# Score products on 64 contraction rows, with q and k turned over unsplit, in an attention and FFN kernel

## The chip, the cores and the metric

One core of a Trainium2 chip runs the whole program. The metric is device time in microseconds of one execution, the median of several runs. TensorE (PE) multiplies and transposes, VectorE (DVE), ScalarE (ACT) and GpSimd (POOL) do the element-wise work, SyncE (SP) issues the DMAs.

## The reference, cut to what matters

Inputs are q, k, v of 2 batches, 8 heads, 768 positions and 64 features, all float32, a projection of 64 x 6, and the weights of two FFNs.

```python
q_bits = (einsum('bhsd,dk->bhsk', q, proj) > 0); k_bits likewise
q_bucket = sum(q_bits * 2**arange(6)); k_bucket likewise
mask = q_bucket[:, :, :, None] == k_bucket[:, :, None, :]
scores = where(mask, q @ k.T / sqrt(64), -1e9)
attn = softmax(scores) @ v                       # per head, 768 x 64
x = attn of all heads side by side               # 1536 x 512
x = leaky_relu(x @ w_in, 0.01) @ w_out           # 512 -> 2048 -> 512
x = (max(h, 0) + alpha * min(h, 0)) @ w_out2     # h = x @ w_in2
```

The result has to be near float32. The kernel gets this from narrower products: a number is held as a rounded high part and the low part that is left, and a product is the sum of high x high, high x low and low x high.

## The kernel before, in words

**Tiles and loops.** The attention goes over 8 pairs of heads (`pairs`, i = 0 to 7). A pair has 12 score tiles, one for each head j of two and each block of 128 query rows (two halves f of three blocks t); a tile is 128 x 768. `TILES` (line 30) is the order of the six (t, j) of a half. The FFNs follow (`ffn`, line 1396); the conversion of their float64 weights (`convert`) runs partly beside the attention.

**The order of the work.** Every step is handed to a planner with a claim (its place in a nominal order), a duration for the planner, what it reads and what it writes (`plan.add`). `Plan.order` lists the steps of each engine by these and improves the order by passes over the whole program; `emit` writes it out. Each engine then runs its own list in order and waits on semaphores. A `ring` is a set of slots that successive buffers take in turn; a buffer waits until the slot's last one has been read.

**A pair's q and k.** `load` (482) brings the two heads of k, q and v, 128 positions on the partitions, 768 numbers each. `split_qk` (542) makes high and low parts ("nat"), by GpSimd for all pairs but the first (lines 470, 473). `turn` (584) transposes them on TensorE (line 597): 128 columns of a head, 64 high and 64 low, become 128 contraction rows, 24 transposes of 128 x 128 for a pair. ScalarE evicts them from PSUM (line 612) into "qa" and "ka", in which the parts lie in opposite order, so that one product over 128 rows gives high x low plus low x high. "qb" and "kb" hold the high parts alone on 64 rows, a copy made by DMA (line 622), and 12 more rows with sign bits.

**The sign bits.** `bits` (631) multiplies the projection (`lhs`, each number and its negative) with the split tiles on 128 rows (line 640): four products side by side on quarters of the columns, for two halves. VectorE compares (line 649), and DMAs lay the bits behind "qb" and "kb" (line 659). For the first pair, copies by the engines stand in for the DMAs (lines 612, 616, 671 and 672). Bits that differ add large terms to the score (`BIG`), which is how the mask enters.

**Scores.** `score` (752) has for each tile two products of 128 rows and two of 76 rows, 384 columns each (line 768), into one of two PSUM slots (`s_ps`). VectorE takes the row minimum and moves the tile to SBUF (line 775), ScalarE takes the exponential (778). Then the tile is turned over: "T" tiles by TensorE (794) and ScalarE (799), the others as high and low halves (812, 818, 470, 473) by a DMA transpose (824). `HI_ON`, `LO_ON` and their `_END` forms say which way each of the 12 tiles takes and which engine does it. `pv` (829) multiplies with v (864, 873) and scales the output (885).

**Buffers.** PSUM has two slots for transposes, bits and others (`t_ps`), one for outputs, one for tiles turned over and two (of two banks each) for scores. The slots of q and k serve the FFN's x later (`op_at`, 952).

Of the kernel before, what the change touches and what calls it, by code (L numbers as in the profile page):

```python
# [18 lines left out]
BIG = 2.0**33  # L19
# [10 lines left out]
TILES = ((0, 0), (2, 0), (0, 1), (1, 0), (2, 1), (1, 1))  # L30
HI_ON = "ATATTTATPATP"
LO_ON = "P-D---P-DP-D"
HI_END, LO_END = "ATATTTATATTT", "P-D---P-D---"
# [17 lines left out]
START, XAT = 10.0, (1, 9)  # L51

# [303 lines left out]
def lsh_attention_ffn_kernel(  # L356
# [66 lines left out]
    op_r = dict(zip(("qa", "qb", "ka", "kb"), ring("op", 4, ("qa", "qb", "ka", "kb"))))  # L423
# [17 lines left out]
    lhs = fixed([128, 32], F32, "lhs")  # L441
    least = fixed([128, 1], F32, "least")
    weight = fixed([128, 1], F32, "weight")
    pj = fixed([128, NB], F32, "pj")
    x_t = {}
# [33 lines left out]
    st_raw, st_nat, st_op, st_bt, st_v = {}, {}, {}, {}, {}  # L479
    sums, pts, st_v32 = {}, {}, {}  # L480

    def load(i, nm, claim, parts=1):
        b, hp = pairs[i]
        src = {"q": q, "k": k, "v": v}[nm][b, 2 * hp:2 * hp + 2]
        t = (rv_r if nm == "v" else raw_r[nm]).new([128, 2, T, D], F32, nm)
        st_raw[nm, i] = t
        for n in range(parts):
            js = slice(2 * n // parts, 2 * (n + 1) // parts)
            plan.add(
                claim,  # L490
                dma(2.4 / parts, lambda js=js: t.t[:, js],
                    lambda js=js: src[js].rearrange("j (p t) d -> p j t d", t=T)),
                writes=[(t, (js.start, js.stop))],
            )

    def setup():
# [8 lines left out]
        def masks():  # L505
            nc.gpsimd.memset(lhs.t, 0.0)
            nc.gpsimd.memset(least.t, 0.0)
            for g in range(4):
                rows = slice(32 * g, 32 * g + 32)
                nc.gpsimd.memset(weight.t[rows], BIG if g % 2 else 1.0)  # L510
                nc.gpsimd.affine_select(
                    out=least.t[rows],
                    in_=least.t[rows],
                    compare_op=ALU.is_ge,
                    fill=-TINY,
                    base=-NB if g % 2 else NB - 1,
                    pattern=[[0, 1]],
                    channel_multiplier=1 if g % 2 else -1,
                )

        plan.add(-98, gps(3.0, masks), writes=[lhs, least, weight])

        def projections():
            for c in range(2):
                gmul(lhs.t[:, NB * c:NB * c + NB], pj.t, -1.0 if c else 1.0)
# [16 lines left out]
    def split_qk(i, parts):  # L542
        for nm, hi, at in (("k", 1, -15), ("q", 0, -13)):
            raw = st_raw.pop((nm, i))
            nat = nat_r[nm].new([128, 2, T, 2, D], F32R, nm + "n")
            st_nat[nm, i] = nat
            for part in range(parts):
                js = slice(2 * part // parts, 2 * (part + 1) // parts)
                u = 1 / parts

                def views(js=js, raw=raw, nat=nat, hi=hi):
                    r = raw.t[:, js].rearrange("p j t d -> p (j t) d")
                    n = nat.t[:, js].rearrange("p j t a d -> p (j t) a d")
                    return n[:, :, hi], n[:, :, 1 - hi], r

                def d_hi(v=views):
                    h, _, r = v()
                    nc.vector.tensor_copy(h, r)

                def a_hi(v=views):  # L560
                    h, _, r = v()
                    nc.scalar.copy(out=h, in_=r)

                def p_hi(v=views):
                    h, _, r = v()
                    gmul(h, r, 1.0)

                def d_lo(v=views):
                    h, lo, r = v()
                    vsub(lo, r, h.bitcast(F32))  # L570

                def p_lo(v=views):
                    h, lo, r = v()
                    gsub(lo, r, h.bitcast(F32))

                span = (js.start, js.stop)
                hi_ways = [vec(0.62 * u + 0.05, d_hi, True), act(0.65 * u + 0.18, a_hi), gps(0.8 * u + 0.05, p_hi)]
                plan.add(12 * i + at, hi_ways if parts > 1 else hi_ways[2], [(raw, span)], [(nat, span)])
                lo_ways = [vec(0.9 * u + 0.05, d_lo, True), gps(1.787 * u + 0.05, p_lo)]
                plan.add(  # L580
                    12 * i + at + 1, lo_ways if parts > 1 else lo_ways[1], [(raw, span)], [(nat, span)]
                )

    def turn(i):
        ops = [{nm: op_r[nm].new([128, S], F32R, nm) for nm in op_r} for j in range(2)]
        st_op[i] = ops
        at = 12 * i - 12
        for nm, hi, sc in (("k", 64, -scale), ("q", 0, 1.0)):
            n = st_nat.pop((nm, i))
            for j in range(2):  # L590
                a, bb = ops[j][nm + "a"], ops[j][nm + "b"]
# [909 lines left out]
```

## Time and profile before

| | |
|---|---|
| Median of 3 runs | 729.72 us (728.97 to 730.33) |
| The profiled execution | 728.91 us, span of its instructions 727.1 us |
| TensorE busy | 708.4 us (97%) |
| VectorE busy | 603.2 us (83%) |
| ScalarE busy | 473.9 us (65%) |
| GpSimd busy | 311.7 us (43%) |
| TensorE's granted clock | full throughout |

Busy times of TensorE count overlapping matmuls once, but each matmul's record is longer than the time after which the next can follow; how far two starts lie apart tells more than the length of one. The chain that ended last follows the work back from the last instruction, at each step to what released it; its shares say which engine the end hangs on. A group of instructions has its busy time, the mean of one, and the idle time of its engine just before it, with what ended that.

### The profile page before, as it was taken

What the parts mean: (1) busy time and instruction counts of PE and PEld (TensorE: products, weight loads), DVE (VectorE), ACT (ScalarE), POOL (GpSimd) and SP (SyncE); (2) the same over time, 40 slices, a digit from 0 to 9 for tenths busy, and PEclk for the clock granted to TensorE, in tenths of its full rate; (3) what the DMA queues carried; (4) which work ended last, traced back from release to release, by engine and by line L of the source; (5) the groups of instructions that cost most, each with busy time, mean ns of one, the idle gap of its engine ahead of it and who ended that gap; (6) DMA issues with size and microseconds to landing.
All of it is one profiled execution on the core that took longest, in us unless ns stands there. A gap on an engine that the chain in (4) does not pass through costs nothing.

```text
span 727.1 us, 13418 instructions
## 1 busy us (share of the span) xinstructions
PE 708.4 (97%) x5113; PEld 461.6 (63%) x5113; DVE 603.2 (83%) x1094; ACT 473.9 (65%) x896; POOL 311.7 (43%) x325
## 2 busy tenths in 40 slices
PE   7999999999998999999999999999999999999997
PEld 5788898888887666666666666555555555555553
DVE  5888887887799989869989878999989999987442
ACT  4888897887897776756656555564776655636340
POOL 1866776868562165132533422424043335323220
PEclk9999999999999999999999999999999999999999
DMA  7457889777565230331322314021132203100012
GB/s 218 109 140 183 166 160 179 173 145 172 118 131 160 87 116 13 106 116 58 103 72 88 95 52 117 6 71 41 59 101 73 88 30 117 58 1 1 24 50 102
DMA packets 103281, 70.86 MB, mean 97 GB/s; under 512 B 72928, under 2 KB 95456, under 8 KB 103216
## 3 DMA queue, kind: packets, MB, share of 16 engines
q1 hardware_dynamic: 103216, 70.00, 36.6%
q8 instruction: 40, 0.66, 0.4%
q14 instruction: 25, 0.20, 0.1%
HBM read 43.00 MB, written 3.15 MB: 63 GB/s over the span
## 4 chain that ended last, share of the span: by engine, by line
PE 72%; DVE 20%; ACT 3%; issue 3%; POOL 1%; DMA 1%; SPq 0%; POOLq 0%; DVEq 0%; ACTq 0%
PE y L1233 10%; PE y L1235 10%; PE y L1234 10%; PE sc L768 7%; PE h L1233 7%; PE h L1234 7%; PE h L1235 7%; PE pp L794 5%; PE o L873 4%; DVE ff L1157 3%; PE o L864 3%; PE tp L597 2%; DVE s L775 2%; DVE ff L1070 2%; DVE x L1367 2%
## 5 line engine op out<-in xcount | busy, mean ns | idle before, releaser
L473 POOL TENSOR_TENSOR ff<-ff 128x384 f16<-128x384 f32 x128 | 137.0, 1084 | 196.8 <-ACT ff L1267 161.1
L1233 PE MATMUL y<-ff 128*128 128x384 f16 (+1 forms) x496 | 172.0, 347 | 0.0
L1235 PE MATMUL y<-ff 128*128 128x384 f16 (+1 forms) x496 | 171.9, 347 | 0.0
L1234 PE MATMUL y<-ff 128*128 128x384 f16 (+1 forms) x496 | 171.9, 347 | 0.0
L1233 PE MATMUL h<-ff 128*128 128x384 f16 x416 | 135.7, 326 | 1.1 <-DVE ff L1278 1.0
L1235 PE MATMUL h<-ff 128*128 128x384 f16 x416 | 135.6, 326 | 0.3 <-DVE ff L1157 0.3
L1234 PE MATMUL h<-ff 128*128 128x384 f16 x416 | 135.6, 326 | 0.0
L1234 PEld LDWEIGHTS <-ff 128*128 128x128 f16 x912 | 89.3, 98 | 69.8 <-issue 2.6
L1235 PEld LDWEIGHTS <-ff 128*128 128x128 f16 x912 | 89.2, 98 | 69.8 <-DVE ff L1157 0.6
L1233 PEld LDWEIGHTS <-ff 128*128 128x128 f16 x912 | 89.2, 98 | 68.3
L775 DVE TENSOR_SCALAR_CACHE_REDUCE s<-sc 128x768 f32<-128x768 f32 x96 | 90.9, 954 | 13.5 <-PE sc L768 10.3
L778 ACT ACTIVATE s<-s,mn 128x768 f32<-128x768 f32 x96 | 90.0, 940 | 8.7 <-DVE s L775 7.6
L1267 ACT CAST ff<-ff 128x384 f16<-128x384 f32 x128 | 64.8, 510 | 28.4 <-DVE ff L1264 26.4
L1367 DVE SCALAR_TENSOR_TENSOR x<-y,back,x 128x384 f32<-128x384 f32 (+1 forms) x84 | 56.2, 670 | 30.1 <-PE y L1235 29.8
L1274 ACT COPY ff<-h 128x384 f32<-128x384 f32 x72 | 34.4, 478 | 49.4 <-PE h L1235 47.9
L799 ACT COPY pt<-pp 128x384 f32<-128x384 f32 x104 | 49.4, 475 | 24.6 <-PE pp L794 23.9
L768 PE MATMUL sc<-ka,qa 128*128 128x384 f32 x192 | 56.9, 377 | 3.1 <-DVE s L775 2.9
L794 PE MATMUL pp<-ident,s 128*128 128x128 f32 x312 | 54.9, 285 | 1.1 <-ACT pt L799 0.6
L470 POOL TENSOR_SCALAR dg<-ident,mx 128x128 fp32r<-128x128 f32 x18 | 11.1, 614 | 104.6 <-DVE mx L1005 74.2
L1157 DVE SCALAR_TENSOR_TENSOR ff<-ff,by 128x512 f16<-128x512 f32 (+2 forms) x54 | 51.5, 970 | 2.7 <-ACT ff L1155 2.6
L1155 ACT ACTIVATE ff<-ff,by 128x512 f16<-128x512 f32 (+2 forms) x54 | 45.4, 872 | 11.1 <-DVE by L1020 5.1
L768 PE MATMUL sc<-kb,qb 76*128 76x384 f32 x192 | 49.8, 339 | 0.6 <-DVE kb L672 0.6
(147 smaller groups left out, 1243.6 us busy)
## 6 DMA issues: line engine op xcount, KB each, us to landing
ff<-in_moe_w_in_dram SPq DMA_DIRECT2D x32, 512.0 KB
ff<-in_moe_w_out_dram SPq DMA_DIRECT2D x32, 512.0 KB
v<-in_v_dram SPq DMA_DIRECT2D x8, 384.0 KB
out_dram<-x SPq DMA_DIRECT2D x12, 256.0 KB
k<-in_k_dram SPq DMA_DIRECT2D x7, 384.0 KB
q<-in_q_dram SPq DMA_DIRECT2D x7, 384.0 KB
kb<-ka SPq DMA_DIRECT2D x14, 192.0 KB
qb<-qa SPq DMA_DIRECT2D x14, 192.0 KB
```

The lines of the kernel that those rows point to most:

```text
L473: nc.gpsimd.tensor_tensor(out=o, in0=a, in1=b, op=ALU.subtract)
L768: nc.tensor.matmul(sc.t[:, h, 0:HALF], lhsT=o[a].t[0:rows, row:row + 128], rhs=o[b].t[0:rows, h * HALF:h * HALF + HALF], start=(n == 0), s ...
L775: plan.add(g, vec(0.965, lambda: nc.vector.tensor_scalar(out=s.t.rearrange("p (a b) -> p a b", a=2), in0=sc.t[:, :, 0:HALF], scalar1=FILL, ...
L778: plan.add(g, act(1.03, lambda: nc.scalar.activation(out=s.t, in_=s.t, func=AF.Exp, scale=-1.0, bias=mn.t[:, 0:1], accum_out=sm.t[:, t, j: ...
L794: nc.tensor.transpose(ps.t[:, c], s.t[:, k0:k0 + 128], ident.t)
L799: act(0.478, lambda ps=ps, out=out: nc.scalar.copy(out=out(), in_=ps.t)),
L1157: plan.add(claim, vec(0.2 + w * 0.00108, lambda: nc.vector.scalar_tensor_tensor(out=part(lo), in0=src(), scalar=c(), in1=part(hi), op0=ALU ...
L1233: nc.tensor.matmul(ps, lhsT=lh[0], rhs=rh[0], start=first, stop=False, skip_group_check=skip)
L1234: nc.tensor.matmul(ps, lhsT=lh[0], rhs=rh[1], start=False, stop=False, skip_group_check=skip)
L1235: nc.tensor.matmul(ps, lhsT=lh[1], rhs=rh[0], start=False, stop=last, skip_group_check=skip)
L1267: plan.add(claim, act(0.51, lambda: nc.scalar.copy(out=gh.ap(), in_=g.ap(F32))), [g.use()], [gh.use()])
L1367: plan.add(claim, vec(0.748 if l else 0.61, lambda: nc.vector.scalar_tensor_tensor(out=a(), in0=ps.ap(w), scalar=c(), in1=a(), op0=ALU.mul ...
```

## The change

- q and k are not split before they are turned over. `load` puts the two heads side by side, 128 numbers of each position, in two DMAs by head (runs of 64 numbers); `turn` makes 12 transposes for a pair instead of 24, whose 128 rows are the two heads' 64 features.
- ScalarE evicts them as a float32 copy ("qr", "kr"); GpSimd makes the high and the low part from that copy (for the first pair VectorE and, for the low part, VectorE or GpSimd). The tiles "nat" and the copies by DMA are gone.
- The sign bits come from the float32 copy: one block of four products for a pair, one comparison, four DMAs of 24 rows. For the first pair four products with all 128 columns and four comparisons write the bits directly. The constants for it are made by VectorE instead of GpSimd.
- `score` makes both heads' tiles of a block of rows in one step: four terms (high-high, low-high, high-low, bits) by two halves of the columns by two heads, 16 products of 64 rows, the heads alternating between rows 0 to 63 and 64 to 127. The step takes both PSUM slots. `TILES` and the strings are reordered, so that a block's two heads follow one another, with as many tiles of each kind in each half as before.
- The planner's claims and durations are those of the new steps. In the FFN, x halves take the slots of "qr", "kr" and the bits instead of "qb" and "kb".

```diff
-TILES = ((0, 0), (2, 0), (0, 1), (1, 0), (2, 1), (1, 1))
-HI_ON = "ATATTTATPATP"
-LO_ON = "P-D---P-DP-D"
+TILES = ((0, 0), (0, 1), (1, 0), (1, 1), (2, 0), (2, 1))
+HI_ON = "AATTTTAPAPTT"
+LO_ON = "PD----PDPD--"
+TURN_AT, BITS_AT, SC, QK_LOAD = -14, -9, 1.57, 2.0
...
-    op_r = dict(zip(("qa", "qb", "ka", "kb"), ring("op", 4, ("qa", "qb", "ka", "kb"))))
+    op_r = dict(zip("qk", ring("op", 4, ("qa", "ka"))))
+    tr_r = dict(zip("qk", ring("tr", 2, ("qr", "kr"))))
...
+            ts = slice(T * n // parts, T * (n + 1) // parts)
+            for j in range(2):
+                plan.add(
+                    claim,
+                    dma(QK_LOAD / parts, lambda ts=ts, j=j: flat(t)[:, ts, 64 * j:64 * j + 64],
+                        lambda ts=ts, j=j: src[j].rearrange("(p t) d -> p t d", t=T)[:, ts]),
...
+    def turn(i):
+        ops = st_op[i] = {nm + x: op_r[nm].new([128, S], F32R, nm + x) for nm in "qk" for x in "hl"}
...
+        at = 12 * i + TURN_AT
+        for nm, sc in (("k", -scale), ("q", 1.0)):
...
+            for f in range(2):
...
+                def go(ps=ps, raw=raw, f=f):
+                    for t in range(TH):
+                        nc.tensor.transpose(
+                            ps.t[:, t * 128:t * 128 + 128], flat(raw)[:, f * TH + t], ident.t)
...
+                plan.add(at, act(0.478, lambda d=dst, s=src, sc=sc: nc.scalar.activation(
+                    out=d(), in_=s(), func=AF.Copy, scale=sc)), [ps], [(r, (f, f + 1))])
+                if i == 0:
...
+            if i:
+                plan.add(at, gps(0.85, lambda hi=hi, r=r: gmul(hi.t, r.t, 1.0)), [r], [hi])
+                plan.add(at + 0.5, gps(1.837, lambda hi=hi, r=r, lo=lo: gsub(lo.t, r.t, hi.t.bitcast(F32))),
+                         [r, hi], [lo])
...
+        plan.add(at, pe(0.785, go), [ops["qr"], ops["kr"], lhs], [ps])
...
-        o = st_op[i][j]
-        sc = s_ps.new([128, 2, 512], F32, "sc")
+        if j == 0:
+            st_sc[i] = [s_ps.new([128, 2, 512], F32, "sc") for _ in range(2)]
+        sc = st_sc[i][j]
...
-            for n, (a, b, rows) in enumerate((("qa", "ka", 128), ("qb", "kb", 64 + NR))):
-                for h in range(2):
-                    nc.tensor.matmul(
-                        sc.t[:, h, 0:HALF], lhsT=o[a].t[0:rows, row:row + 128],
-                        rhs=o[b].t[0:rows, h * HALF:h * HALF + HALF],
-                        start=(n == 0), stop=(n == 1),
-                    )
-        plan.add(g - 1, pe(0.785, go), [o[a] for a in op_r], [sc])
+                for n, (a, c) in enumerate(("hh", "lh", "hl", "bb")):
+                    for h in range(2):
+                        for k in range(2):
+                            rows = slice(64 * k, 64 * k + 64)
+                            nc.tensor.matmul(
+                                both[k].t[:, h, 0:HALF], lhsT=o["q" + a].t[rows, row:row + 128],
+                                rhs=o["k" + c].t[rows, h * HALF:h * HALF + HALF],
+                                start=(n == 0), stop=(n == 3),
+                            )
+            plan.add(g - 1, pe(SC, go), reads, both)
...
-        split_qk(i, 1 if i else 2)
```

## Rows read from the trace of the kernel before

**Rows 1.** The page: busy us of TensorE (share, instructions), and the chain by engine
```profile
PE 708.4 (97%) x5113; PEld 461.6 (63%) x5113; DVE 603.2 (83%) x1094; ACT 473.9 (65%) x896; POOL 311.7 (43%) x325
PE 72%; DVE 20%; ACT 3%; issue 3%; POOL 1%; DMA 1%; SPq 0%; POOLq 0%; DVEq 0%; ACTq 0%
```

**Rows 2.** Stretches (from:to length): busy us (instructions) by engine, clock, DMA share, GB/s
```profile
15.00:45.00 30.00, 26.87 (x240) 21.97 (x240) 24.98 (x52) 22.97 (x51) 18.93 (x17) 1.00 0.43 112
139.10:165.30 26.20, 26.19 (x277) 22.15 (x277) 20.82 (x45) 21.28 (x48) 19.56 (x20) 1.00 0.78 171
191.60:255.00 63.40, 59.84 (x601) 46.10 (x601) 59.78 (x123) 51.23 (x98) 22.31 (x25) 1.00 0.48 121
```

**Rows 3.** The chain of waits from 139 to 166 us: start, length, what
```profile
by line: PE sc L768 32.5%; PE pp L794 18.9%; PE o L873 14.6%; PE o L864 12.8%; PE tp L597 10.5%; PE bp L640 8.6%; PE pr L847 2.5%; PE vp L705 0.2%; issue 0.0%
...
139.16 0.78 PE bp L640 x8
...
153.31 1.42 PE sc L768 x8
...
165.36 0.76 PE bp L640 x5
```

**Rows 4.** TensorE in order of time: start, length, line, out<-in, shapes, count
```profile
112.21 0.49 PE L597 MATMUL tp<-ident,qn 128*128 128x128 f32 x3
112.63 0.51 PE L640 MATMUL bp<-qa,lhs 128*32 128x384 f32 x1
...
112.65 0.51 PE L640 MATMUL bp<-ka,lhs 128*32 128x384 f32 x1
112.98 0.49 PE L640 MATMUL bp<-qa,lhs 128*32 128x384 f32 x1
...
113.42 0.62 PE L768 MATMUL sc<-ka,qa 128*128 128x384 f32 x2
113.88 0.51 PE L768 MATMUL sc<-kb,qb 76*128 76x384 f32 x2
```

**Rows 5.** The same view, transposes one after another: six in 0.65 us
```profile
118.58 0.49 PE L597 MATMUL tp<-ident,kn 128*128 128x128 f32 x3
118.91 0.49 PE L794 MATMUL pp<-ident,s 128*128 128x128 f32 x3
119.23 0.96 PE L597 MATMUL tp<-ident,kn 128*128 128x128 f32 x6
```

**Rows 6.** Waits: who waited for whom, us in total, times, longest
```profile
DVE s L775 <- PE sc L768: 10.3, 33, 0.9
PEld sc L768 <- DVE s L775: 6.4, 15, 1.7
```

**Rows 7.** Groups of VectorE from 139.1 to 165.3 us: busy us, mean ns, idle before
```profile
L775 DVE TENSOR_SCALAR_CACHE_REDUCE s<-sc 128x768 f32<-128x768 f32 x12 | 11.4, 956 | 2.8 <-PE sc L768 1.9 <-POOL hl L473 0.8
L818 DVE SCALAR_TENSOR_TENSOR hl<-s,hl 128x768 f16<-128x768 f32 x3 | 2.9, 954 | 0.9 <-ACT hl L812 0.9
L649 DVE TENSOR_SCALAR bt<-bp,least,weight 128x384 f32<-128x384 f32 x2 | 1.4, 676 | 1.6 <-PE bp L640 1.6
```

**Rows 8.** Groups of the whole span: evictions, GpSimd's subtraction, VectorE's of the first pair
```profile
L612 ACT ACTIVATE qa<-tp 128x384 fp32r<-128x384 f32 x32 | 15.7, 497 | 3.0 <-PE tp L597 3.0
L473 POOL TENSOR_TENSOR kn<-k,kn 128x768 fp32r<-128x768 f32 x7 | 13.5, 1930 | 0.5
L616 DVE TENSOR_SCALAR ka<-tp 128x384 fp32r<-128x384 f32 x2 | 1.1, 553 | 0.7 <-ACT kb L612 0.7
L476 DVE TENSOR_TENSOR kn<-k,kn 128x384 fp32r<-128x384 f32 x2 | 1.0, 550 | 0.0
```

**Rows 9.** All engines in order of time, the first 22 us
```profile
2.00 1.06 SPq L467 DMA_DIRECT2D k<-in_k_dram  x2
...
4.65 0.51 ACT L562 CAST kn<-k 128x384 fp32r<-128x384 f32 x1 [2.65 <-DMA k<-in_k_dram]
...
17.00 0.44 PE L768 MATMUL sc<-kb,qb 76*128 76x384 f32 x1 [0.58 <-DVE kb L672]
...
19.02 0.95 DVE L775 TENSOR_SCALAR_CACHE_REDUCE s<-sc 128x768 f32<-128x768 f32 x1
```

**Rows 10.** TensorE in order of time: pair 7's first score
```profile
203.12 0.60 PE L768 MATMUL sc<-ka,qa 128*128 128x384 f32 x2
```

**Rows 11.** The chain of waits at the last scores
```profile
220.12 0.89 DVE s L775 x2
221.01 0.04 issue
221.06 0.96 PE sc L768 x4
```

More of the change, by code (lines that the diff above doesn't have):

```diff
@@ L440, in lsh_attention_ffn_kernel @@
     inv = fixed([128, NP], F32, "inv")
-    lhs = fixed([128, 32], F32, "lhs")
-    least = fixed([128, 1], F32, "least")
+    lhs = fixed([128, 128], F32, "lhs")
+    least = fixed([128, 3], F32, "least")
     weight = fixed([128, 1], F32, "weight")
     pj = fixed([128, NB], F32, "pj")
+    bit_r = dict(zip("qk", ring("bit", 2, ("qb", "kb"))))
+    bit = {(nm, n): part(bit_r[nm], n).new([128, S], F32R, nm + "b") for nm in "qk" for n in range(2)}
     x_t = {}
@@ L476, in vsub @@
         nc.vector.tensor_tensor(out=o, in0=a, in1=b, op=ALU.subtract)
-    st_raw, st_nat, st_op, st_bt, st_v = {}, {}, {}, {}, {}
+    st_raw, st_op, st_sc, st_v = {}, {}, {}, {}
     sums, pts, st_v32 = {}, {}, {}
@@ L505, in masks, with steps @@
         def masks():
[L506 to L521, printed above, removed]
+            v = nc.vector
+            v.memset(lhs.t, 0.0)
+            v.memset(least.t, 0.0)
+            v.memset(weight.t, 1.0)
+            def steps(c, r0, *marks):
+                for n, r in enumerate(marks):
+                    v.memset(least.t[r0:r0 + r, c:c + 1], 0.0 if n % 2 else -TINY)
+            steps(0, 32, 32, 32 - NB)
+            steps(0, 64, NR, NB)
+            steps(1, 32, 32 - NB, 32 - NR)
+            steps(1, 64, NB)
+            for r0 in (0, 64):
+                steps(2, r0, 2 * NR, NR + NB, NR, NB)
+                steps(2, r0 + 32, NR + NB, NR, NB)
+                v.memset(weight.t[r0 + 32:r0 + 64], BIG)
+        plan.add(-98, vec(2.5, masks), writes=[lhs, least, weight])
+        for nm in "qk":
+            plan.add(-3, gps(0.7, lambda nm=nm: nc.gpsimd.memset(bit[nm, 1].t.bitcast(F32), 0.0)), writes=[bit[nm, 1]])
         def projections():
-            for c in range(2):
-                gmul(lhs.t[:, NB * c:NB * c + NB], pj.t, -1.0 if c else 1.0)
+            for c in range(4):
+                rows, c0 = slice(64 * (c // 2), 64 * (c // 2) + 64), 64 - NR + NB * c
+                gmul(lhs.t[rows, c0:c0 + NB], pj.t[rows], -1.0 if c % 2 else 1.0)
             nc.gpsimd.tensor_scalar(
@@ L540, in warm @@
             plan.add(-50, pe(0.9, go), [ident], [b, fill])
-    def split_qk(i, parts):
-        for nm, hi, at in (("k", 1, -15), ("q", 0, -13)):
-            raw = st_raw.pop((nm, i))
[L545 to L581, printed above, removed]
-                )
@@ L951, in lsh_attention_ffn_kernel @@
     OPS = [(nm, k) for nm in ("qa", "qb", "ka", "kb") for k in range(4)]
-    op_at = {key: on(op_r[key[0]], key[1], S) for key in OPS}
+    op_at = {(nm, k): on(op_r[nm[0]], k, S) for nm, k in OPS if nm[1] == "a"}
+    for nm in "qk":
+        for n in range(2):
+            op_at[nm + "b", 2 * n] = on(bit_r[nm], n, S)
+            op_at[nm + "b", 2 * n + 1] = on(tr_r[nm], n, S)
     nat_at = {nm: on(nat_r[nm], 0, 2 * S) for nm in "kq"}
```

158 lines of the change are left out of this document (62 added, 96 removed).

## The prediction

> **What bounds the kernel now.** Read first the page's shares and its chain that ended last [rows 1]: TensorE is busy nearly all the time and carries 72% of the chain, VectorE 20%. The busy time by stretches [rows 2] says where which of them holds. In one whole period of a head pair (139.1 to 165.3 us) TensorE has no idle time at all, while VectorE has 20.8 of 26.2 us, ScalarE 21.3 and GpSimd 19.6: there only TensorE work counts. At the start (15 to 45 us) no engine is full, and the tail of the attention (191.6 to 255 us) is VectorE's, 59.8 of 63.4 us. The chain of waits in that period [rows 3] confirms it: every piece is PE, one after the other, and the two bit products that open two periods lie 26.2 us apart. The chain gives scores the largest share, 32.5%, so this change rebuilds the costliest item of the stage that TensorE bounds. What comes after 255 us is untouched but for buffers: the FFN's x halves take the same kinds of slots under new names, and those of a batch come free no later.
>
> **The sum's base** is the profiled execution, 728.9 us (span 727.1 and 1.8 around it), 0.8 under the median of the runs shown.
>
> **Score matmuls.** Now a tile and head takes four matmuls of 384 columns; eight run in 1.42 us, 0.177 each [rows 3]. The change makes sixteen of 64 rows for two heads where eight of 128 and 76 rows stood. If the two row halves run at once, that is eight steps of 0.177, the same 1.42 us. No row of before has a product on half the rows. The nearest is the bit product on column quarters: its first and fourth matmul start 0.02 us apart and its next pass 0.35 after the first, so packed products do run side by side [rows 4]. I take full overlap by that row; the other end is none at all: 96 steps per pair instead of 48, 48 x 0.177 = 8.5 us more for each pair.
>
> **Changing the array's shape.** The same rows price it. Three transposes start at 112.21 and at 0.108 each [rows 5] are through at 112.53; the bits start at 112.63: 0.10 late. Passes follow at 0.35, but the scores start 0.44 after the last: 0.09. And the first two score matmuls take 0.46, where two take 0.35: 0.11 for a weight load that nothing hides [rows 4]. A score block of its own shape would pay the three, 0.30. Now it has the shape of its neighbours and pays none; after, six blocks a pair pay 6 x 0.30 = 1.8 us. The ends are 0 and 1.8, and I take 1.8 by the row. The Trainium skill (TensorEngine Tiling (Array Packing), Key Properties) speaks against the change in the same way: a change of tiling mode drains the engine. By that rule 1.8 holds for row tiles too, without it the sum would be 1.8 better per pair; the trace agrees for column tiles and is silent on row tiles.
>
> **Transposes and bits.** q and k go over unsplit with both heads on the rows: 12 transposes a pair instead of 24, 12 x 0.108 = 1.3 us less [rows 5]. One bit product instead of two: from 112.53 to 113.53 (113.88 less two matmuls at 0.177) a block costs 1.0 us [rows 4], so 1.0 less. PE per pair: -1.3 - 1.0 + 1.8 = -0.5 us.
>
> **Other engines.** ScalarE loses four evictions of 0.497 a pair, VectorE one bit comparison of 0.676, and GpSimd keeps the two rounds and two subtractions a pair, now behind the eviction instead of ahead of the transposes [rows 7, 8]. SP loses four copies of 192 KB and gains two load issues; its transposes queue behind less. All this lies under TensorE's 26 us and counts nothing by itself. The loads are cut into runs of 256 bytes; they are due some 20 score steps ahead and the DMA engines have a share of 0.78 [rows 2], so nothing; if that cover were gone, the transposes of the next pair would wait, with every score behind them in TensorE's order. The raw tile, free after the transposes instead of after GpSimd's subtraction, covers for it.
>
> **The new wait.** Both heads' scores are now one block that needs both PSUM slots empty, and VectorE gets them together. Queued behind that wait are the transposes, products and outputs on TensorE; behind VectorE's wait for the block are its halves, outputs and weight conversion. The loop: 1.42 + 0.30 for the block, 0.88 + 0.96 for the two minima (0.956 for one alone, 0.89 where two follow) [rows 7, 11], some 0.3 of handing over (estimate; 0.04 of it is the issue time in rows 11): 3.9 us. A period of 25.7 has six loops of 4.3. So it fits with 0.4 us to spare per block. Today TensorE's score waits on a minimum are short and few [rows 6]. I take 0, with bounds 0 and 0.5 per block.
>
> **The start.** The first score block ended late: its last sign product waited until 17.00 us, and the first minimum ran at 19.02 [rows 9]. Sixteen evictions of 0.5, four subtractions, and the bits' casts stand before it; after, for the first block k needs two transposes, two rounds, two subtractions and two comparisons, and q half as many: nine VectorE steps of 0.55 to 0.68 [rows 7, 8]. The first half of k was there 2.1 us after its issue (2.00 to 2.53, half of two issues of 1.06; the cast that reads it at 4.65) [rows 9]. With six issues of 0.53, four for k and two for half of q, the last of them lands at 2.0 + 3.2 + 2.1 = 7.3; VectorE can start at about 5.7, when the second issue has landed and is turned over, and is through at about 11. Block 1.7, so the first minimum near 13, 6 us earlier. Not all of it stays: between 15 and 45 us VectorE is busy for 25 of 30 us [rows 2] with work that remains. I take 4.5, bounds 1 and 7.
>
> **The tail.** VectorE loses one comparison; pair 7's scores spread over 18.6 us (203.12 to 221.68, the last matmul of the block of 221.06) [rows 10, 11], under six loops of 3.9 (23.4 less the first wait). They may start earlier, VectorE has conversion work to fill the gaps. I take 0, bounds -1 and +3.
>
> **Sum.** I count 5.5 periods for pairs 1 to 6, half a one off for stretches that VectorE leads (it has 20% of the chain [rows 1]): 5.5 x 0.5 = 2.8. With 4.5 at the start: -7.3, 728.9 - 7.3 = 721.6. **Forecast 722 us**, 1.0% faster; its own range 715 to 729.
>
> **The rivals.**
> *Free change of shape.* The row blocks start with no drain: 5.5 x 1.8 = 9.9 less, 712. For it: a row half uses the same columns. Against: both shape changes of rows 4 cost 0.1. Chance 0.10.
> *The start gives nothing.* VectorE's remaining work, not the operands, sets when pair 0 ends: 728.9 - 2.8 - 1 = 725 at best and 728 with a small stall. For it: 25 of 30 us busy; against: 5 idle ones. Chance 0.13, 727.
> *The coupled block stalls TensorE (slower).* A VectorE instruction of about 0.95 us, such as L818 [rows 7], that is under way when a block ends eats the 0.4 and leaves TensorE idle for 0.55. It decides when it eats the whole gain of 7.3, at 13 of the 36 blocks of pairs 1 to 6; with 18 of them, and the 3 of the tail, 13 more, 735. For it: today the two slots alternate, tile by tile, and hide just this. Against: VectorE's work besides the minima, (20.8 - 11.4) / 6 = 1.6 us a block [rows 2, 7], fits into the 1.7 us for which a block runs. Chance 0.20.
> *The two row halves' weights load one after the other (slower).* An unhidden load took 0.11; two are 0.22 where a step has 0.177: 48 x 0.043 = 2.1 us per pair, 7 pairs 14: 736. For it: every matmul here has its own load; against: in rows 4 four matmuls with their loads start within 0.02 us. Chance 0.10. The Trainium skill (TensorE: Matmul & The Clock Gate, Part 3) reports 3.07 times for four row tiles rather than 4; by that estimate a step would take 0.177 x 4 / 3.07 = 0.23, and the time would be some 740; no run here shows it yet.
> *No overlap at all*, the change doesn't do what it says: 8 x 8.5 = 68 more, 790. Chance 0.05.
>
> **How the numbers follow.** Forecast 0.42, then 0.10, 0.13, 0.20, 0.10 and 0.05. This kernel's measurement can tell 0.2%, 1.5 us. Faster by more: 0.39 of the forecast, 0.10, 0.09 of the start rival and 0.02 of the stalls: 0.60. Within: 0.02 + 0.03 + 0.05 = 0.10. Slower: 0.30. The range runs from 712 to 738: it leaves out no overlap (0.05), the upper ends of the two slower cases (0.08) and half of the free change (0.05).
>
> **What would show it.** In the changed trace: the two heads' score matmuls start within 0.01 us of each other and pairs follow at 0.18 (0.22: weights in turn; 0.18 for single ones: no overlap). Between transposes and a score block about 0.2 instead of 0.11. First minimum near 13 us. The distance of the pairs' first scores 25.7 us instead of 26.2. TensorE's idle time on a minimum: under 0.1 per block by the forecast, 0.3 and more by the stall rival. The forecast is wrong if the periods don't shrink while TensorE idles before score blocks, or if the first minimum comes early and pair 1 doesn't.

## The result, and the profile after

The changed kernel took 736.44 us (median of 3 runs, 735.50 to 736.57) where the kernel before took 729.72: a ratio of 1.0089, 95% interval 1.0066 to 1.0112. It is slower by 6.7 us; the forecast was 722 us.

The page of the changed kernel, the same two lines as [rows 1]:

```profile
PE 710.3 (97%) x5353; PEld 456.7 (62%) x5353; DVE 604.6 (82%) x1101; ACT 467.4 (64%) x870; POOL 310.6 (42%) x311
PE 74%; DVE 17%; ACT 5%; issue 2%; POOL 1%; POOLq 0%; ACTq 0%
```

By sums hardly anything moved: TensorE has 2 us more, VectorE 1. The loss doesn't show as work of an engine, so the stretches have to tell where it is. The span grew from 727.1 to 733.7 us. First the start, on VectorE and TensorE (start, length, line, out<-in, shapes, count):

```profile
14.46 0.95 DVE L741 TENSOR_SCALAR_CACHE_REDUCE s<-sc 128x768 f32<-128x768 f32 x1
```

```profile
12.04 0.62 PE L733 MATMUL sc<-kh,qh 64*128 64x384 f32 x4
...
32.54 0.50 PE L733 MATMUL sc<-kb,qb 64*128 64x384 f32 x4
...
43.56 0.62 PE L733 MATMUL sc<-kh,qh 64*128 64x384 f32 x4
...
208.43 0.61 PE L733 MATMUL sc<-kh,qh 64*128 64x384 f32 x4
```

The same view of the kernel before, its pair 1 (pair 7 is in [rows 10]):

```profile
44.45 0.60 PE L768 MATMUL sc<-ka,qa 128*128 128x384 f32 x2
```

The first minimum ran at 14.46 instead of 19.02 [rows 9], 4.6 us earlier. But pair 0's scores then spread over 20.7 us (12.04 to 32.72, the last start in the group of 32.54) where before they took 17.2, and pair 1 began only 0.9 us earlier. From pair 1's first score to pair 7's it is 164.9 us, before 158.7: six periods of 27.48 instead of 26.45, 6.2 us lost. From pair 7's first score to the end it is 525.3 us, before 524.0: 1.3 lost. Together -0.9 + 6.2 + 1.3 = +6.6, the growth of the span.

The busy time of the stretch from pair 1's first score to pair 7's (columns as in [rows 2]), first of the kernel before, then of the changed one:

```profile
44.45:203.12 158.67, 157.81 (x1683) 134.04 (x1682) 131.88 (x284) 132.91 (x293) 115.16 (x112) 1.00 0.77 166
```

```profile
43.56:208.43 164.87, 156.42 (x1831) 126.62 (x1830) 136.88 (x276) 128.14 (x272) 110.22 (x105) 1.00 0.66 125
```

TensorE is busy for 1.4 us less, as the change meant, but it now idles for 164.87 - 156.42 = 8.4 us, 1.41 a pair, where it idled for 0.9 in all, 0.14 a pair. The granted clock is 1.00 in both rows. VectorE is busy for 5.0 us more, with eight instructions fewer: some of its steps got longer, which the last section takes up. What ended TensorE's idle time (its waits in this stretch: us in total, times, longest), after and then before:

```profile
PE pp L760 <- ACT pt L765: 5.8, 13, 0.8
PE sc L733 <- DVE s L741: 2.4, 4, 1.0
```

```profile
PE sc L768 <- DVE s L775: 0.6, 1, 0.6
PE pp L794 <- ACT pt L799: 0.2, 1, 0.2
```

And of the waits of the whole span the one that answers to the first of [rows 6], with the weight loads' wait for ScalarE:

```profile
DVE s L741 <- PE sc L733: 19.1, 25, 1.5
...
PEld pp L760 <- ACT pt L765: 19.0, 35, 1.1
```

Two of TensorE's waits have grown: for the minimum, and, larger, for ScalarE to empty the one bank in which exponentials are turned over. On its side VectorE waits almost twice as long for scores as before (19.1 us against 10.3 [rows 6]), in fewer and longer pieces. Both engines wait for each other more, as in a round trip that no longer overlaps.

One such stall in order of time. TensorE:

```profile
105.45 0.55 PE L760 MATMUL pp<-ident,s 128*128 128x128 f32 x3
105.92 0.62 PE L733 MATMUL sc<-kh,qh 64*128 64x384 f32 x4
106.38 0.52 PE L733 MATMUL sc<-kh,ql 64*128 64x384 f32 x4
106.74 0.52 PE L733 MATMUL sc<-kl,qh 64*128 64x384 f32 x4
107.09 0.50 PE L733 MATMUL sc<-kb,qb 64*128 64x384 f32 x4
107.53 0.55 PE L760 MATMUL pp<-ident,s 128*128 128x128 f32 x3
...
109.77 0.55 PE L760 MATMUL pp<-ident,s 128*128 128x128 f32 x3
111.28 0.44 PE L733 MATMUL sc<-kh,qh 64*128 64x384 f32 x1 [0.97 <-DVE s L741]
112.16 0.44 PE L733 MATMUL sc<-kh,qh 64*128 64x384 f32 x2 [0.44 <-DVE s L741]
```

VectorE in the same time:

```profile
104.20 0.95 DVE L741 TENSOR_SCALAR_CACHE_REDUCE s<-sc 128x768 f32<-128x768 f32 x1
105.08 0.08 DVE L741 DVE_READ_ACCUMULATOR s<-sc 128x1 f32 x1
105.08 1.56 DVE L784 SCALAR_TENSOR_TENSOR hl<-s,hl 128x768 f16<-128x768 f32 x1
106.56 0.86 DVE L680 TENSOR_SCALAR vb<-v,c 128x768 f16<-128x768 f32 x1
107.46 2.45 DVE L688 SCALAR_TENSOR_TENSOR vb<-v,c,vb 128x768 f16<-128x768 f32 x1
...
110.27 0.95 DVE L741 TENSOR_SCALAR_CACHE_REDUCE s<-sc 128x768 f32<-128x768 f32 x1
111.14 0.08 DVE L741 DVE_READ_ACCUMULATOR s<-sc 128x1 f32 x1
111.14 0.95 DVE L741 TENSOR_SCALAR_CACHE_REDUCE s<-sc 128x768 f32<-128x768 f32 x1
```

The block of both heads ends at about 107.5 and fills both slots. VectorE is then in a lump of other work, 105.08 to 110.27, and takes the first minimum 2.8 us later, the second 0.9 after that. TensorE has used up what lay between the blocks by 110.3, and there is no third slot. It idles 0.97, begins the block with the first head's product alone at 111.28 and stops again until the second slot is empty (112.16). ScalarE gets its two exponentials one behind the other too, after 2.67 us without work:

```profile
108.11 0.48 ACT L765 COPY pt<-pp 128x384 f32<-128x384 f32 x1 [1.49 <-PE pp L760]
111.26 0.94 ACT L744 ACTIVATE s<-s,mn 128x768 f32<-128x768 f32 x1 [2.67 <-DVE s L741]
112.10 0.19 ACT L744 ACTIVATION_READ_ACCUMULATOR s<-s,mn 128x1 f32 x1
112.19 0.92 ACT L744 ACTIVATE s<-s,mn 128x768 f32<-128x768 f32 x1
```

A lump by itself is nothing new. In the kernel before VectorE takes no minimum from 52.64 to 58.91 us and is busy with other work for 5.4 of that; TensorE, which has other work there too, doesn't idle (columns as in [rows 2]):

```profile
52.64:58.91 6.27, 6.27 (x96) 5.72 (x93) 5.44 (x14) 5.10 (x15) 4.03 (x5) 1.00 0.62 142
```

### The profile page after: what moved, and what is told of

It reads as the page before. It is cut to its first block, busy times and chain, and to the rows that moved or that the text cites. A ratio compares the mean times of both kernels' runs of the same rounds, so it can differ in the third digit from the quotient of the medians.

```text
span 733.7 us, 13780 instructions
## 1 busy us (share of the span) xinstructions
PE 710.3 (97%) x5353; PEld 456.7 (62%) x5353; DVE 604.6 (82%) x1101; ACT 467.4 (64%) x870; POOL 310.6 (42%) x311
## 4 chain that ended last, share of the span: by engine, by line
PE 74%; DVE 17%; ACT 5%; issue 2%; POOL 1%; POOLq 0%; ACTq 0%
PE y L1203 10%; PE y L1205 10%; PE y L1204 10%; PE sc L733 9%; PE h L1203 7%; PE h L1205 6%; PE h L1204 6%; PE pp L760 5%; DVE ff L1127 5%; PE o L839 4%; PE o L830 2%; ACT pt L765 2%; DVE ff L1040 2%; ACT s L744 1%; DVE ff L1033 1%
## 5 line engine op out<-in xcount | busy, mean ns | idle before, releaser
L741 DVE TENSOR_SCALAR_CACHE_REDUCE s<-sc 128x768 f32<-128x768 f32 x96 | 88.1, 954 | 24.5 <-PE sc L733 19.1
L760 PE MATMUL pp<-ident,s 128*128 128x128 f32 x312 | 56.6, 290 | 11.0 <-ACT pt L765 10.4
L1127 DVE SCALAR_TENSOR_TENSOR ff<-ff,by 128x512 f16<-128x512 f32 (+2 forms) x54 | 53.0, 1012 | 2.0 <-ACT ff L1125 2.0
L760 PEld LDWEIGHTS pp<-ident,s 128*128 128x128 f32 x312 | 32.5, 141 | 33.2 <-ACT pt L765 19.0
L839 PE MATMUL o<-pt,v 128*64 128x128 f32 x624 | 50.2, 273 | 0.0
L1043 DVE SCALAR_TENSOR_TENSOR ff<-ff 128x1024 int32<-128x1024 int32 (+1 forms) x36 | 42.9, 1193 | 0.7
```

The costliest lines, as they stand in the source:

```text
L741: plan.add(g, vec(0.965, lambda: nc.vector.tensor_scalar(out=s.t.rearrange("p (a b) -> p a b", a=2), in0=sc.t[:, :, 0:HALF], scalar1=FILL, ...
L760: nc.tensor.transpose(ps.t[:, c], s.t[:, k0:k0 + 128], ident.t)
L839: nc.tensor.matmul(ps.t[64 * j:64 * j + 64, t * 128:t * 128 + 128], lhsT=v32.t[:, j, c, :], rhs=whole(pt, t)[:, T * j + c], start=(c + t = ...
L1127: plan.add(claim, vec(0.2 + w * 0.00108, lambda: nc.vector.scalar_tensor_tensor(out=part(lo), in0=src(), scalar=c(), in1=part(hi), op0=ALU ...
```

## The experiments

The theory: the row halves make one block of two tiles, which needs both PSUM slots empty and gives VectorE and ScalarE their work in twos; this coupling alone costs more than the change saves. The rivals: the new order of tiles, a plan laid out for too short a block, longer steps of VectorE beside GpSimd's, the one bank for turned exponentials.

The measured numbers of all runs stand in one table. "Pair 0" is the time from its first score's start to its last; "pair 1" is the start of its first score; "period" is a sixth of the time from there to pair 7's first score; "idle" is that time less TensorE's busy time, per pair. Ratios are to the kernel before as it ran beside each of them. It took 729.7 to 730.7 us, so a difference of 1 us between runs that didn't stand side by side says nothing.

| run | us (lowest to highest) | ratio, 95% | pair 0 | pair 1 | period | idle |
|---|---|---|---|---|---|---|
| before | 729.72 (728.97 to 730.33) | | 17.2 | 44.45 | 26.45 | 0.14 |
| changed | 736.44 (735.50 to 736.57) | 1.0089, 1.0066 to 1.0112 | 20.7 | 43.56 | 27.48 | 1.41 |
| b_coupled | 739.19 (738.05 to 740.78) | 1.0135, 1.0112 to 1.0158 | 21.7 | 43.99 | 27.70 | 0.62 |
| b_order | 726.18 (725.61 to 726.85) | 0.9951, 0.9936 to 0.9966 | 17.5 | 42.61 | 26.74 | 0.39 |
| b_order_again | 725.66 (725.13 to 727.39) | 0.9946, 0.9934 to 0.9958 | 17.6 | 41.79 | 26.61 | 0.30 |
| b_coupled_order | 737.56 (735.69 to 739.08) | 1.0100, 1.0079 to 1.0122 | 25.8 | 46.92 | 27.61 | 0.85 |
| a_two_single | 718.86 (718.07 to 720.87) | 0.9855, 0.9835 to 0.9874 | 16.2 | 45.90 | 24.05 | 1.22 |
| a_two_coupled | 734.22 (733.61 to 735.49) | 1.0063, 1.0047 to 1.0080 | 19.9 | 42.50 | 27.31 | 2.78 |
| a_sc175 | 739.12 (737.49 to 739.87) | 1.0117, 1.0096 to 1.0137 | 25.3 | 48.37 | 27.08 | 1.08 |
| a_no_low | 733.05 (732.63 to 733.42) | 1.0040, 1.0025 to 1.0055 | 20.9 | 44.50 | 26.79 | 0.96 |
| b_no_low | 724.63 (723.98 to 725.02) | 0.9926, 0.9913 to 0.9939 | 15.8 | 42.82 | 26.25 | 0.20 |
| a_two_pp | 735.37 (735.01 to 737.62) | 1.0077, 1.0058 to 1.0096 | 19.5 | 44.00 | 26.72 | 0.96 |
| b_two_pp | 751.58 (749.62 to 755.57) | 1.0299, 1.0262 to 1.0337 | 18.9 | 56.64 | 28.52 | 1.90 |
| a_no_low_two_pp | 736.86 (736.01 to 737.46) | 1.0087, 1.0070 to 1.0104 | 19.2 | 44.93 | 26.80 | 1.07 |

### Coupling alone, and order alone

b_coupled is the kernel before with its own products, but one step for two consecutive tiles:

```diff
+        if m % 2 == 0:
+            st_sc[i] = [s_ps.new([128, 2, 512], F32, "sc") for _ in range(2)]
+        sc = st_sc[i][m % 2]
...
+                for n, (a, b, rows) in enumerate((("qa", "ka", 128), ("qb", "kb", 64 + NR))):
+                    for h in range(2):
+                        for sc_, o_, row_ in both:
...
-        plan.add(g - 1, pe(0.785, go), [o[a] for a in op_r], [sc])
+            plan.add(g - 1, pe(1.57, go), [o_[a] for _, o_, _ in both for a in op_r], [x[0] for x in both])
```

> The kernel before with one edit: two tiles that follow one another in the order are made by one step of eight products (128 and 76 rows, as before) that takes both PSUM slots; transposes, bits, order of tiles and shapes stay. Coupling theory (VectorE has to empty both slots before TensorE can begin the next block): TensorE idles before score blocks, a pair's period grows from 26.2 to 27 or 28 us, pair 0's twelve scores take about 20 us instead of 17.3, pair 7's about 22 instead of 18.6, and the time is 735 to 743 us. Order theory (tiles in T-T runs wait for the one slot of turned tiles) and port theory (GpSimd's subtractions slow VectorE): no change, 728 to 731.

b_order is the kernel before with the four lines of order:

```diff
-TILES = ((0, 0), (2, 0), (0, 1), (1, 0), (2, 1), (1, 1))
-HI_ON = "ATATTTATPATP"
-LO_ON = "P-D---P-DP-D"
-HI_END, LO_END = "ATATTTATATTT", "P-D---P-D---"
+TILES = ((0, 0), (0, 1), (1, 0), (1, 1), (2, 0), (2, 1))
+HI_ON = "AATTTTAPAPTT"
+LO_ON = "PD----PDPD--"
+HI_END, LO_END = "AATTTTAATTTT", "PD----PD----"
```

> The kernel before with the changed kernel's order of tiles and its strings of ways alone. Order theory: TensorE waits on ScalarE's eviction of turned tiles as in the changed kernel, 734 us or more. Coupling theory: no change beyond what a new plan scatters, 727 to 732.

b_coupled_order has both edits.

> The kernel before with the coupling alone (one step of eight products fills both slots for two consecutive tiles) and with the changed kernel's order of tiles and of the engines that turn the exponentials over, in which the two tiles of a step are the two heads of one tile of queries. If coupling and order add up, it stands 3.6 us under the run with the coupling and the old order (739.2), at 735 to 737 us, and 9 us or more over the run with the new order alone (726.2). If the coupling only hurt because the old order pairs tiles badly, it falls to 727 to 731 us.

Coupling alone made the kernel before 9.4 us slower, as the coupling theory had it (only pair 7's scores spread further than it said, 24.6 us). Order alone made it 3.6 us faster, which neither theory expected: 726.18 is just under the 727 to 732 of the one and far under the 734 of the other. With both it stood 11.4 over the run with the order alone, more than the 9 expected; but it came only 1.6 us under the run with the coupling alone, so the two don't simply add up. In both twins the coupling lengthens pair 0 (17.2 to 21.7, 17.5 to 25.8) and the period (by 1.25 and 0.87). VectorE's waits for scores in b_coupled show the same as in the changed kernel, 23.9 us where [rows 6] has 10.3:

```profile
DVE s L784 <- PE sc L777: 23.9, 23, 4.1
```

Its stretch from pair 1 to pair 7 (columns as in [rows 2]):

```profile
43.99:210.19 166.20, 162.49 (x1678) 135.26 (x1676) 128.24 (x273) 138.60 (x304) 106.42 (x105) 1.00 0.70 152
```

VectorE isn't busier there than in the kernel before (128.24 us against 131.88, with 11 instructions fewer), so the loss of b_coupled needs no longer work of VectorE.

One sign is weaker than in the changed kernel: idle time grew by 0.48 a pair, where the period lost 1.25. The rest is in gaps too short to count as idle, since a matmul's record is longer than the distance to the next. From start to start, what exceeds the usual distance grew over the six periods, which lost 7.5 us, by 2.9 us in front of turned exponentials and by 2.5 in front of q's and k's transposes; the share of the score blocks depends on what is taken as usual for them. So the coupling theory holds in its sum. The order is no cause of the loss; in the kernel before, with the plan that it gets there, it is a gain.

Because it beats both kernels, b_order ran once more:

> The kernel before with the changed kernel's order of tiles and of the engines that turn the exponentials over, once more and in more rounds: 725.5 to 727 us, 0.4 to 0.6% under the kernel before, if the order's gain is one of its own.

It took 725.66 us, 0.54% under the kernel before (0.42 to 0.66%): the best full kernel here is the kernel before with only the changed order. As the program is the same, this confirms its time and not that every plan with this order would have it.

### The change with and without its coupling

Two versions of the changed kernel make a block of 128-row products without row halves. They leave out two of the four terms and sum the two others over both heads' rows, so the scores are other numbers; TensorE has eight steps for two tiles, as many as the row halves need, and no change of shape. In a_two_single each tile is its own step with its own slot; in a_two_coupled both tiles are one step, and this is its edit:

```diff
-                for n, (a, c) in enumerate(("hh", "lh", "hl", "bb")):
+                for n, (a, c) in enumerate(("hh", "bb")):
...
-                            rows = slice(64 * k, 64 * k + 64)
...
-                                both[k].t[:, h, 0:HALF], lhsT=o["q" + a].t[rows, row:row + 128],
-                                rhs=o["k" + c].t[rows, h * HALF:h * HALF + HALF],
+                                both[k].t[:, h, 0:HALF], lhsT=o["q" + a].t[:, row:row + 128],
+                                rhs=o["k" + c].t[:, h * HALF:h * HALF + HALF],
...
```

> The changed kernel with each tile's scores in a step and a slot of its own, and two of the four terms left out, over all 128 rows (so the output is another one): 0.70 us for a tile as before, no coupling and no change of shape for scores; transposes, bits and order as changed. Coupling theory: the savings of transposes and bits come through, periods of about 24 us, start 4 us earlier, 710 to 719 us. Order or port theory: periods stay above 26 us and the time above 725.

> As the run with single tiles, with two of the four terms over 128 rows, but in one step for both heads that takes both slots, as in the changed kernel: the coupling stays, the change of the array's shape (0.3 us a block by my sum, 1.8 us a pair) goes. If the shape's price bounds the pairs, 726 us; if the coupling's wait takes its place, 731 to 737, and the distance to the run with single tiles, 15 us and more, is the coupling's.

With the same products the coupled twin is 15.4 us slower (718.86 and 734.22). The first of them is what the change would be worth on this schedule if its tiles could stay apart and the shape were free: 11.0 us under the kernel before, in which the gain of the order (3.6 us in b_order) is contained. The second shows that the changes of shape, which I counted at 1.8 us a pair, are by now worth only some 736.44 - 734.22 = 2.2 us in all (the intervals of the two ratios overlap, so it can be less): without them TensorE idles 2.78 us a pair instead of 1.41. What TensorE saves, it waits. The busy times (columns as above), a_two_single first:

```profile
45.90:190.20 144.30, 136.99 (x1362) 114.10 (x1361) 126.42 (x261) 117.99 (x258) 109.29 (x107) 1.00 0.67 136
```

```profile
42.50:206.34 163.84, 147.17 (x1545) 126.82 (x1544) 141.52 (x275) 126.84 (x270) 110.44 (x104) 0.99 0.64 127
```

A caution on these: a_two_single has 183 fewer matmuls in the stretch, because more of pair 0's products ran ahead of pair 1 and more of the last ones behind pair 7's first score. So its period of 24.05, which the coupling theory had named, and its late pair 1, which it had expected 4 us earlier, are partly a shift of work; the 15.4 us, of the whole program, are not.

### A plan for a longer block

```diff
-TURN_AT, BITS_AT, SC, QK_LOAD = -14, -9, 1.57, 2.0
+TURN_AT, BITS_AT, SC, QK_LOAD = -14, -9, 1.75, 2.0
```

> The changed kernel with one number of the planner changed: a score block is priced at 1.75 us instead of 1.57 when the order of the work is laid out, so that the other engines' steps are placed for a block as long as the trace shows it with its changes of shape (1.42 + 0.30). The theory that the order was laid out for a block that is too short, so that the stalls are a fault of placement, expects 728 to 733 us and an idle TensorE under 1.2 us per pair. The coupling theory, by which any order has to fit VectorE's steps of 0.9 to 2.4 us between two pairs of minima, expects no gain: 735 to 740 us, idle 1.5 us per pair or more.

The time went the coupling theory's way (739.12). The periods went half the other way: 27.08 instead of 27.48, idle 1.08 a pair, under the bound of 1.2 that the placement theory set. What that gave, the start took: pair 0 spread over 25.3 us and pair 1 began at 48.37, 4.8 us later. Placement moves the loss about; with this plan it doesn't remove it.

### GpSimd's subtractions

In a_no_low GpSimd scales by zero where it subtracted:

```diff
-                plan.add(at + 0.5, gps(1.837, lambda hi=hi, r=r, lo=lo: gsub(lo.t, r.t, hi.t.bitcast(F32))),
+                plan.add(at + 0.5, gps(0.85, lambda hi=hi, r=r, lo=lo: gmul(lo.t, r.t, 0.0)),
```

> The changed kernel, but GpSimd's two subtractions for the low parts of q and k (1.7 to 2.1 us each) are each one scaling by zero of about 0.9 us: the low parts are left out, they are zeros. The score block, its two slots and all waits stay. The coupling theory (two slots filled by one block, emptied by two minima, leave TensorE without the next block when VectorE is late) expects at most a small gain, 733 to 737 us, and an idle TensorE of 1.3 us per pair or more between the first scores of pairs 1 and 7. The rival, that GpSimd's longer work beside VectorE stretches VectorE's steps (the conversion of 2.45 us that lay beside such a subtraction) and makes the minima late, expects most of the loss to go: 724 to 730 us, TensorE idle under 0.6 us per pair.

b_no_low does the same in the kernel before (line 579).

> The kernel before, with GpSimd's two subtractions for the low parts of q and k (1.8 to 1.9 us each) replaced from the second pair on by one scaling by zero each: the low parts are left out, they are zeros. It is the control for the same cut in the changed kernel, which gave 3.4 us. If VectorE's longer steps beside those subtractions cost time only where a block waits for both slots, the kernel before loses nothing by them: 728 to 731 us. If they cost every order of the work the same, 725 to 727 us.

Both got faster, the changed kernel by 3.4 us and the kernel before by 5.2, so neither expectation of the control held as written. Nor did one of a_no_low's hold whole: its time is at the lower end of the coupling theory's 733 to 737, its idle time, 0.96 a pair, lies between the 1.3 of that theory and the 0.6 of the rival. For the total it is clear enough: without the subtractions the two kernels stand 8.4 us apart (733.05 and 724.63), with them 6.7. They cost both kernels something and do not make the difference. In the six periods alone they count for more in the changed kernel: 4.1 us (27.48 to 26.79 each) against 1.2 (26.45 to 26.25), so that of the 6.2 us which the periods lost 3.2 are left without them. Longer lumps of VectorE thus add to the coupling's loss there; the kernel before has the rest of its gain in pair 0 and at the end. In a_no_low the waits for minima are gone from TensorE's list, and the one for evictions stays (the same stretch, pair 1 to pair 7):

```profile
PE pp L760 <- ACT pt L765: 5.5, 12, 0.7
```

### A second bank for the turned exponentials

```diff
-    t_ps = ring("ps_t", 2, space=PSUM)
+    t_ps = ring("ps_t", 1, space=PSUM)
...
-    p_ps = ring("ps_p", 1, space=PSUM)
+    p_ps = ring("ps_p", 2, space=PSUM)
```

> The changed kernel with its PSUM banks dealt out otherwise: two for the turned exponentials (one before) and one for the transposes, bits and row sums (two before). All work and the coupled score block stay. Between the first scores of pairs 1 and 7 TensorE idles 8.4 us in the changed kernel, 5.8 of it in front of the turning of exponentials, until ScalarE has emptied the one bank. If that wait is one of its own, which the coupled block makes because two exponentials of 0.9 us come to ScalarE at once and the evictions stand behind them, a second bank takes it: 729 to 732 us, idle under 0.6 us per pair. If it only passes on that the minima are late, the idle time moves to the score blocks and the time stays at 735 to 738 us.

> The kernel before with the same banks (two for the turned exponentials, one for the transposes, bits and row sums). Its TensorE idles 0.9 us in all between the first scores of pairs 1 and 7, so a second bank has nothing to give: 728 to 733 us, and what it stands over the kernel before is the price of the single bank for transposes and bits. If it is faster by 3 us or more, a second bank helps any order of the work and the other run says nothing of the coupled block.

> The changed kernel with both: the low parts of q and k left out (one GpSimd scaling by zero in place of each subtraction) and two banks for the turned exponentials. With the low parts left out alone the run took 733.0 us, with 5.5 us of idle TensorE left in front of the turned exponentials between the first scores of pairs 1 and 7 and none in front of score blocks. If the waits for minima and for evictions are two separate losses, both are gone here: 726 to 729 us, idle under 0.4 us per pair. If they are one loss in two places, it stays above 731 us.

In a_two_pp the wait for evictions is gone, and another has come (TensorE's waits from pair 1 to pair 7):

```profile
PE sc L733 <- DVE s L741: 3.3, 5, 1.3
PE bp L620 <- DVE c L669: 1.9, 4, 0.6
```

The periods are 0.76 us shorter, 4.6 in all, and the end gave it back: from pair 7's first score to the end it is 531.3 us, 6.0 more. All of that lies between pair 7's first score and its last, 28.1 us instead of 22.1; why it does with one bank for transposes and bits stays open. The control missed both of its expectations: in the kernel before this deal of banks costs 21 us, with TensorE idle for 1.90 us a pair, its granted clock at 0.97 in that stretch and pair 1 at 56.64. So the second bank's gain in the periods of the changed kernel is no general one, but the runs can't price the wait for evictions alone. The run with both edits (736.86) missed the 726 to 729 of two separate losses: its period, 26.80, is that of either edit alone (26.79, 26.72), and the wait for minima, which had gone from TensorE's list in a_no_low, is back:

```profile
PE sc L733 <- DVE s L741: 3.7, 6, 1.3
```

That speaks for one loss in two places, and isn't proof of it, since the single bank for transposes and bits has a price of its own in the control. None of these edits got below some 26.7 us a pair, with about one of them idle.

## Why the prediction was wrong

**What bounds.** Right in the main: TensorE's order sets the time, and its chain share went from 72 to 74%. The tail was read by half: its row in [rows 2] has TensorE as busy as VectorE (59.84 and 59.78 us of 63.40), so it doesn't show that VectorE leads there.

**Score matmuls.** Right. The two heads' matmuls start together (one pair at 157.131 and 157.135 us), and groups of four, two such pairs, follow at 0.35 to 0.36 (106.38, 106.74, 107.09). That rules out no overlap (0.70) and weights in turn (0.44).

**Changing the array's shape.** Right in its size. From the start of the last transpose before a block to that of the first after it, an undisturbed block takes 1.81 us here and, with the eight full-row steps of a_two_coupled, 1.52 (medians over their traces): 0.29, where I said 0.30. The split was off: the block starts 0.20 us after the last transpose's start, before it was 0.03 and not the 0.11 that I gave; the first group of four takes 0.46 against 0.35, but in a_two_coupled it takes 0.43 too; and 107.09 plus 0.35 is followed at 107.53, 0.09 late. The price of the rule I set against the change (the Trainium skill, TensorEngine Tiling (Array Packing), Key Properties: a change of mode drains the engine) thus holds for row tiles too. It was wrong in its weight: by the runs it is some 2.2 us of the total, not 9.9, because TensorE waits anyway.

**Transposes, bits and other engines.** Right as far as it can be seen: TensorE is busy for 0.23 us less a pair, with the small gaps counted as busy, where I said 0.5. That the other engines' work counts nothing was wrong: VectorE's steps got longer beside GpSimd's (last section).

**The new wait: the step that failed.** I took 0. From pair 1 to pair 7 TensorE idles 8.4 us, 0.23 for each of 36 blocks, inside the bounds of 0 to 0.5 that I gave and far from the value that I took. Two things were wrong in it. I compared a loop of 3.9 us with a mean of 4.3 and called the difference slack; and I set VectorE's other work against it as an average, 1.6 us a block. The rows of the stall show lumps instead: 5.2 us from one pair of minima to the next where 1.7 fit, and nothing to catch up with afterwards, since TensorE had no second slot to run ahead into. The kernel before idled 0.9 us in its stretch, and it has lumps as long (52.64 to 58.91); so by these rows a lump costs where the next block needs both slots and TensorE has no other work left. The loop itself was not under-counted, although of its 0.3 for handing over only 0.04 stood in a row: the nearest blocks of the changed trace start 3.20 us apart (139.16 and 142.36). From 139 to 167 us VectorE's conversions are those of [rows 7] and others, and longer (busy us, mean ns):

```profile
L784 DVE SCALAR_TENSOR_TENSOR hl<-s,hl 128x768 f16<-128x768 f32 x3 | 3.6, 1213 | 1.3 <-ACT hl L778 1.3
L688 DVE SCALAR_TENSOR_TENSOR vb<-v,c,vb 128x768 f16<-128x768 f32 x2 | 3.5, 1728 | 0.0
```

I had also looked at one place only where a late minimum would show, in front of the scores. ScalarE, which gets its exponentials in twos, passes the delay on to TensorE's turned exponentials; that is 5.8 of the 8.4 us.

**The start.** Mis-sized: 4.5 taken, 0.9 measured. The first minimum did come 4.6 us earlier (14.46; I said 13). Pair 0's first score came 3.6 us earlier (12.04, before 15.65), its last only 0.2 (32.72, before 32.90): six blocks at 3.45 us each, where the tiles of before took 17.2 in all. I had applied the loop to the later pairs and the tail, not to the one stage where no engine was full and so nothing else would hide it. VectorE took pair 0's last minimum 3.3 us earlier than before (36.94 and 40.23), and even so pair 1 began only 0.9 earlier. Against pair 1 as a mark speaks that a_two_single, with pair 0 through at 28.22, has it at 45.90; where the start's gain would have gone without the coupling stays open.

**The tail.** Within its bounds (-1 to +3): 1.3 lost, with pair 7's scores spread over 22.1 us instead of 18.6.

**The rivals.** The coupled block that stalls TensorE was the one, at 735 us with a chance of 0.20. Its mechanism was the right one, and its place half: 17 stalls of 0.18 to 0.97 us from pair 1 to pair 7, four in front of scores and 13 in front of turned exponentials, and a start that gave next to nothing. The rival of the start alone (727) was right in its size and not enough.

**How sure this is.** Every edit makes the planner lay out the whole program anew, and edits that have nothing to do with the coupling moved the time by 3 to 5 us (order, subtractions). The coupling's price of 9.4, 11.4 and 15.4 us in three pairs of runs stands well over that; the split of the 6.7 us into single causes does not.

## What to carry to other kernels

When a packing of the array ties two output tiles into one step, count the slots: two that alternated become one that doesn't, and the producer's run-ahead is gone. Compare the round trip then not with the mean time per block but with the longest lump of other work on the consuming engines between two blocks, and ask whether the producer has enough other work to put there; and look for the delay at every place where the producer waits for those engines. An engine that is busy for 97% of the time gains nothing from less work if the new step makes it wait for others.

## What the runs showed of the hardware

VectorE's conversions from SBUF to SBUF wait for the whole of a GpSimd instruction that is under way when they begin. In the stall above GpSimd ran:

```profile
104.17 1.66 POOL L477 TENSOR_TENSOR hl<-s,hl 128x768 f16<-128x768 f32 x1
105.78 1.23 POOL L806 TENSOR_SCALAR rb<-sum 128x384 f32<-128x384 f32 x1
106.98 2.12 POOL L477 TENSOR_TENSOR ql<-qr,qh 128x768 fp32r<-128x768 f32 x1
```

The first ends at 105.83 and VectorE's step from 105.08, which has two SBUF inputs, at 106.64; the third ends at 109.10 and VectorE's step from 107.46, another with two, at 109.91. Both end 0.81 us after GpSimd's, a little under the length of such a step elsewhere (0.954 [rows 7]). The step with one SBUF input between them waited too: it ends at 107.42, 0.41 us after GpSimd's second instruction, and took 0.86, where the mean of its line is 0.61 with the subtractions of q and k left out (a_no_low). Beside a longer instruction of GpSimd the same line took 2.18 and ended at 53.96, again 0.41 us after it:

```profile
51.01 2.54 POOL L477 TENSOR_TENSOR ql<-qr,qh 128x768 fp32r<-128x768 f32 x1
...
51.78 2.18 DVE L680 TENSOR_SCALAR vb<-v,c 128x768 f16<-128x768 f32 x1
```

The minima, which read PSUM, keep their 0.95 throughout. With the subtractions of q and k left out, the mean of all eight conversions of line 688 fell from 1372 to 1075 ns. For the steps with two inputs the Trainium skill says so (SBUF — State Buffer, Who interferes with whom): whichever of the two issues second is blocked until the first has finished, and a VectorE step with two SBUF inputs takes part in this; the trace agrees. I had taken GpSimd's work as lying beside VectorE's at no cost. The kernel before has such waits as well: its conversions of exponentials take 1007 ns in the mean of the whole span, those of the changed kernel 1399. b_order, which has the changed kernel's order alone, has 1356 and is the faster kernel, so longer conversions by themselves don't explain the loss.
